# A fused retention and SoLU kernel: the negated row and its maximum taken early for the softmax, squares on ScalarE, new orders

## The chip, the cores and the metric

The kernel runs on one core of a Trainium2 chip. The metric is the device time of one execution in microseconds (us), as the median of repeated runs. The engines are named as in the profile: PE is TensorE's matmul (PEld its weight load), DVE is VectorE, ACT is ScalarE, POOL is GpSimd, and SP is the SyncE queue, which issues nearly all DMAs. SBUF is the working memory on the chip, PSUM the memory into which PE writes.

## The reference

Two layers, one behind the other. The first is a retention layer (8 batches, 8 heads, 576 positions, head size 64), the second a feed-forward layer with a SoLU activation over all 4608 tokens (512 to 1024 to 512):

```
scores = (q @ k.T) / 8                      # per batch and head
ret    = scores * Dmat                      # Dmat[i, j] = gamma_h ** (i - j) for i >= j, else 0
x      = (ret @ v), heads side by side      # 4608 x 512
h      = x @ w_in                           # 4608 x 1024
e      = exp(h - max(h));  sm = e / (sum(e) + 1e-9)
solu   = h * sm
ln     = (solu - mean) / sqrt(var + 1e-6) * g_ln
out    = ln @ w_out                         # 4608 x 512
```

All inputs and outputs are float32.

## The kernel before

**Tiling.** The positions are cut into windows. For each group of four batches there are eight windows of 256 positions (`wi` 0 and 1 of each batch), and one window that holds the last 64 positions of the four batches. That makes 18 windows. Each is worked on twice, for heads 0 to 3 and for heads 4 to 7, which makes 36 *units* (index i). Each window also gives two *token tiles* of 128 tokens, so there are 36 tiles (index t) as well. One unit and one tile make one step of a software pipeline.

**One unit.** SP loads q, k and v as float32 (`ldq`, `ldk`, `ldv`, lines L259 and L266). POOL multiplies q and k by the decay factors and casts them to float16 (`sq`, `sk`, L274) and casts v (`cv`, L282); in the first two units DVE scales q and ACT casts v. PE transposes q and k (`T`, L291), ACT copies them out of PSUM (`qe`, L299). PE forms the scores (`S`, L349), and DVE multiplies them by the causal mask into `ret` (`mask`, L382). The state that goes from chunk to chunk is formed by PE (`K`, L314), two additions on DVE (`sa` and `sd`, L396 to L403), a product and two casts on POOL (`sm` L407, `sc` L416). PE adds the part of earlier chunks (`I`) and of the own chunk (`V`, both L314) in the PSUM tile `xy`, and ACT copies it out as `xT` (`xe`, L422).

**One tile.** PE multiplies xT by w_in into `h_ps`, two banks of PSUM with one buffer (`M1`, L434). ACT takes the exponential and its row sum straight from `h_ps` (`ex`, L447); no maximum is subtracted. DVE multiplies `h_ps` by `e_sb` into `solu` in float16 (`so`, L454), which releases `h_ps`. The softmax's divisor is not divided out: as the layer norm divides by the standard deviation, it only appears in the epsilon. DVE forms mean and variance of `solu` (`bn`, L460 and L464) and, once a window, var + 1e-6 * sum² (L468 and L471, named `w`); POOL raises it to the power -1/2 (`rs`, L477). PE transposes `solu` (`L`, L483), ACT copies it out (`le`, L491), and PE multiplies it by w_out (`M2`, L507). ACT scales the result by `rs` (`oe`, L523) and SP stores it (`out`, L535 and L542).

**The mean.** There are two ways of taking out the mean. Tiles below `NE` (14) use `w2g16`, g times w_out, and DVE corrects the result: `od` (L515) adds the mean times the negative column sums of the weights, `nws`. From tile 14 on, the weights themselves are centred: `w2c16`, made by ACT (`wf`, L657) and POOL (`wp`, L578) in eight pieces, and `od` is left out. The column sums come from a matmul with a matrix of -1 (`WM`, L574), copied out twice by ACT (`nw0`, `nw1`, L665).

**Order.** Each engine works through its queue in order. The order of each queue is written out by hand in `FIRST` for the first part; after that operations come by a due time of period 5.36. `order_ops` merges the five lists into one order of emission, with planned durations from `DUR` and with the number of buffers from `CAP`. Where the plan sees PE idle early on, the kernel emits matmuls on zeros (`wm`, L687 and L694) that keep PE busy.

Of the kernel before, what the change touches and what calls it, by code (L numbers as in the profile page):

```python
# [9 lines left out]
FP = mybir.dt.float32  # L10
F16 = mybir.dt.float16
P = 128
# [4 lines left out]
    qe=0.6, xe=0.59, ex=1.22, le=0.6, oe=0.69, wi=0.6, wg=0.66, cva=0.6,  # L17
    mask=1.22, st_a=0.29, so=1.22, bn=1.68, od=0.7, wib=0.55, wgd=0.5, WM=1.73, nw=0.62, wf=0.66, wp=1.04, sqd=0.7, gc=0.2,
    sq=1.03, sk=1.03, st_b=0.4, cast=0.84, rs=0.6, cv=0.61,
# [6 lines left out]
NE = 14  # L26

FIRST = dict(
    ACT=(
        "cv0 qe0 cv1 qe1 xe0 wi1a wi2a wi0a xe1 wi3a ex0 qe2 wg0 le0 wg2 qe3 wg4 wg6 ex1 xe2 "  # L30
        "nw1 nw0 xe3 qe4 wf1 ex2 qe5 wf3 le1 xe4 qe6 wf2 ex3 le2 xe5 oe0 qe7 wf0 ex4 le3 xe6 "
        "qe8 ex5 le4 xe7 qe9 oe1 ex6 le5 oe2 qe10 xe8 ex7 le6 xe9 qe11 oe3 ex8 le7 oe4 wf6 "
        "qe12 xe10 wf4 ex9 le8 xe11 oe5 wf7 qe13 ex10 le9 xe12 wf5 qe14 oe6 ex11 le10 xe13 "
        "oe7 qe15 oe8 ex12 le11 xe14 qe16 oe9 ex13 le12 xe15 qe17 oe10 ex14 le13"
    ),
    DVE=(
        "gc sq0 sa0 sd0 sq1 mask0 wi1b sa1 sd1 mask1 wi2b wi0b wi3b sa2 sd2 so0 mask2 wg1 sa3 "
        "sd3 wg3 wg5 wg7 mask3 so1 bn0 sa4 sd4 bn1 mask4 so2 od0 sa5 sd5 mask5 bn2 sa6 sd6 "
        "so3 mask6 od1 bn3 sa7 sd7 so4 mask7 od2 bn4 sa8 sd8 so5 mask8 bn5 sa9 sd9 so6 od3 "
        "mask9 bn6 so7 od4 sa10 sd10 mask10 bn7 so8 od5 sa11 sd11 mask11 bn8 sa12 so9 sd12 "  # L40
        "od6 mask12 bn9 sa13 sd13 so10 od7 mask13 bn10 so11 sa14 sd14 od8 bn11 mask14 so12 "
        "sa15 sd15 od9 mask15 bn12 so13 od10 mask16 bn13 so14"
    ),
    PE=(
        "G K0 T0 S0 T1 I0 V0 K1 S1 I1 V1 M1_0 T2 K2 S2 L0 I2 V2 K3 T3 M1_1 S3 WM I3 V3 K4 T4 "
        "M1_2 S4 T5 M2_0 L1 I4 V4 K5 S5 T6 M1_3 I5 V5 K6 S6 L2 M2_1 T7 M1_4 I6 V6 K7 S7 L3 "
        "M2_2 T8 M1_5 I7 V7 K8 S8 L4 M2_3 T9 M1_6 I8 V8 K9 L5 S9 T10 M1_7 L6 I9 M2_4 V9 K10 "
        "S10 T11 M1_8 L7 I10 M2_5 V10 K11 S11 T12 M1_9 L8 I11 V11 K12 S12 M2_6 T13 M1_10 I12 "
        "V12 K13 S13 L9 M2_7 T14 M1_11 I13 L10 M2_8 V13 K14 S14 T15 M1_12 L11 M2_9 I14 V14 "
        "K15 S15 T16 M1_13 L12 I15 S16 V15 M2_10 T17 M1_14 L13 I16 S17 V16 M2_11"  # L50
    ),
    POOL=(
        "sk0 sk1 sm0 sc0 sm1 sc1 sq2 sk2 cv2 sk3 sm2 sc2 cv3 sq3 sm3 sc3 sk4 sq4 cv4 sq5 sk5 "
        "sm4 sc4 sq6 rs0 cv5 sk6 sq7 sm5 sc5 cv6 cv7 sk7 sm6 sk9 sc6 sk8 sq8 wp0 rs1 sm7 sc7 "
        "cv8 sq9 cv10 cv9 wp3 sm8 sk10 sc8 cv12 wp2 sq10 sq11 sq12 sm9 sc9 sk11 cv11 sk12 wp1 "
        "sm10 sc10 sk13 rs2 sq13 sq14 cv14 sm11 sc11 sk14 rs3 wp6 sm12 sc12 cv13 sq16 cv15 "
        "cv16 sm13 sc13 wp4 sk15 sq15 sk16 wp5 rs4 sm14 sc14 sq17 wp7 sk17 rs5 cv17 sm15 sc15 "
        "sq18 sk18 cv18 sq19 sk19 cv19"
    ),
    SP=(  # L60
        "ldk0 ldv0 ldq0 ldk1 ldq1 lm ldv1 lwi1 lwi2 lwi0 lwi3 ldq2 ldk2 ldv2 ldk3 lwo0 ldv3 "
        "ldq3 lwo2 lwo4 lwo6 ldk4 ldq4 ldv4 ldq5 ldk5 ldq6 ldv5 ldk6 ldv7 ldq7 ldq9 ldk7 ldk8 "
        "ldv6 ldq10 ldv8 ldk9 ldq11 ldq8 ldv10 ldk10 ldv11 ldq14 ldk11 ldk14 ldv9 ldv12 ldq12 "
        "ldk12 ldk13 ldq16 out0 out1 ldk17 ldv16 ldq15 ldq13 ldv13 out2 ldv14 ldq17 ldk16 "
        "out4 ldv15 ldk15 out3 out5 out7 out6 ldv17 ldv18 ldq19 ldk18 ldv19 ldq18 ldk19 ldq20 "
        "out8 ldk20 ldv20 out9 ldq21 ldk21 ldv21"
# [107 lines left out]
def kernel(  # L174
# [21 lines left out]
               xT=5, h=1, e=2, oc=2, solu=3, sml=8, lnT=4, o=1, osb=3)  # L196
# [28 lines left out]
    nws = const.tile([P, 2, DM], FP)  # L225
# [213 lines left out]

    def exp_(t):  # L440
        d = tk[t]
        w, c = divmod(t, 2)
        d["e"] = pools["e"].tile([P, DFF], FP, tag="e", name="e_sb")
        if c == 0:
            ws[w]["se"] = pools["sml"].tile([P, 2], FP, tag="se", name="se")
            ws[w]["mv"] = pools["sml"].tile([P, 2, 2], FP, tag="mv", name="mv")
        nc.scalar.activation(  # L447
            out=d["e"], in_=d["h"], func=ACT.Exp, accum_out=ws[w]["se"][:, c : c + 1]
        )

    def solu(t):
        d = tk[t]
        d["solu"] = pools["solu"].tile([P, DFF], F16, tag="solu", name="solu")
        nc.vector.tensor_tensor(out=d["solu"], in0=d["h"], in1=d["e"], op=ALU.mult)  # L454

    def stats(t):
        w, c = divmod(t, 2)
        bs = pools["sml"].tile([P, 2, 6], FP, tag="bs", name="bs")
        for half in range(2):
            nc.vector.bn_stats(  # L460
                out=bs[:, half], in_=tk[t]["solu"][:, half * 512 : half * 512 + 512]
            )
        d = ws[w]
        nc.vector.bn_aggr(out=d["mv"][:, c], in_=bs)  # L464
        if c:
            x = pools["sml"].tile([P, 2], FP, tag="w", name="w")
            d["x2"] = pools["sml"].tile([P, 2], FP, tag="w2", name="w2")
            nc.vector.scalar_tensor_tensor(  # L468
                out=x, in0=d["se"], scalar=1e-6, in1=d["se"], op0=ALU.mult, op1=ALU.mult
            )  # L470
            nc.vector.tensor_tensor(out=d["x2"], in0=x, in1=d["mv"][:, :, 1], op=ALU.add)  # L471
# [39 lines left out]
    def o_mean(t):  # L511

        d = tk[t]
        d["oc"] = pools["oc"].tile([P, DM], FP, tag="oc", name="oc")
        nc.vector.scalar_tensor_tensor(  # L515
            out=d["oc"], in0=nws[:, 0], scalar=ws[t // 2]["mv"][:, t % 2, 0:1], in1=d["o"],
            op0=ALU.mult, op1=ALU.add,
        )
# [58 lines left out]
    def w2_center(x):  # L577
        nc.gpsimd.tensor_tensor(out=w2c16[:, x], in0=w2_f[:, x], in1=nws[:, 1], op=ALU.add)  # L578
# [46 lines left out]
    for t in range(NT):  # L625
        w, c = divmod(t, 2)
        m = t + 2
        op(f"M1_{t}", "PE", "M1", [f"xe{2 * w}", f"xe{2 * w + 1}"] + [f"wi{x}{y}" for x in range(4) for y in "ab"],
           (m, 3.18), lambda t=t: mm1(t), [("h", [f"so{t}"])])
        op(f"ex{t}", "ACT", "ex", [f"M1_{t}"], (m, 5.1), lambda t=t: exp_(t), [("e", [f"so{t}"])])  # L630
        op(f"so{t}", "DVE", "so", [f"ex{t}"], (m + 1, 1.03), lambda t=t: solu(t), [("solu", [f"L{t}", f"bn{t}"])])
        op(f"bn{t}", "DVE", "bn", [f"so{t}", f"bn{t - 1}" if c else ""], (m + 1, 4.5), lambda t=t: stats(t))
        if c:
            op(f"rs{w}", "POOL", "rs", [f"bn{t - 1}", f"bn{t}"], (m + 2, 0.77), lambda w=w: rstd(w), [("sml", [f"oe{t}"])])
        op(f"L{t}", "PE", "L", [f"so{t}"], (m + 1, 4.9), lambda t=t: ln_tp(t), [("tp", [f"le{t}"])])
        op(f"le{t}", "ACT", "le", [f"L{t}"], (m + 2, 0.97), lambda t=t: ln_ev(t), [("lnT", [f"M2_{t}"])])
        o_end = f"od{t}" if t < NE else f"oe{t}"
        op(f"M2_{t}", "PE", "M2", [f"le{t}"] + [f"{'wg' if t < NE else 'wp'}{x}" for x in range(8)], (m + 4, 1.0),
           lambda t=t: mm2(t), [("s" if late(t) else "o", [o_end])])
        if t < NE:  # L640
            op(o_end, "DVE", "od", [f"M2_{t}", "nw0"], (m + 4, 2.9), lambda t=t: o_mean(t), [("oc", [f"oe{t}"])])
        op(f"oe{t}", "ACT", "oe", [o_end if t < NE else f"M2_{t}", f"rs{w}"], (m + 4, 3.6 if t < NE else 2.9),
           lambda t=t: o_ev(t), [("osb", [f"out{t}"])])
        op(f"out{t}", "SP", "out", [f"oe{t}"], (m + 4, 4.4 if t < NE else 3.6), lambda t=t: store(t))
# [8 lines left out]
    op("gc", "DVE", "gc", ["G"], (0, 1.0), lambda: nc.vector.tensor_copy(out=gln, in_=cur["g_ps"][:, 0:8]))  # L653
    for c in range(0, 8, 2):
        op(f"lwo{c}", "SP", "ldw", [], (-2 + c / 8, 0.6), lambda c=c: nc.sync.dma_start(out=w2_f[:, c : c + 2], in_=w2_v[:, c : c + 2]))
        for x in (c, c + 1):
            op(f"wf{x}", "ACT", "wf", ["gc", "nw1"], (8 + x * 0.75, 1.9), lambda x=x: nc.scalar.activation(  # L657
                out=w2_f[:, x], in_=w2_f[:, x], func=ACT.Copy, scale=gln[:, x : x + 1]))
            op(f"wp{x}", "POOL", "wp", [f"wf{x}"], (9 + x * 0.75, 1.9), lambda x=x: w2_center(x))
# [3 lines left out]
    op("WM", "PE", "WM", [f"wg{x}" for x in range(8)], (5, 1.0), w2_sum, [("tp", ["nw0", "nw1"])])  # L663
    for x in range(2):
        op(f"nw{x}", "ACT", "nw", ["WM"], (5, 1.1), lambda x=x: nc.scalar.activation(  # L665
            out=nws[:, x], in_=cur["w_sum"], func=ACT.Copy, scale=1.0 if x == 0 else 1.0 / DFF))
# [7 lines left out]
    with tc.manual_schedule():  # L674
# [4 lines left out]
        nc.vector.memset(minus1, -1.0)  # L679
# [3 lines left out]
        nc.vector.memset(warm, 0.0)  # L683
# [43 lines left out]
```

## Time and profile before

| | us |
|---|---|
| median of 3 runs | 226.4 |
| the runs | 227.62, 225.35, 226.40 |
| span of the profiled execution, first to last instruction | 225.6 |
| PE busy | 208.6 |
| DVE busy | 180.0 |
| POOL busy | 151.6 |
| ACT busy | 133.2 |

The profile gives the span of the one execution that was profiled and no other time of it; the median of the runs lies 0.8 us above that span. Busy times are shares of one engine's own time, overlaps counted once. The mean duration of one instruction can be a little longer than the distance from its start to the next one's: neighbours overlap by some hundredths of a microsecond.

### The profile page before, as it was taken

How to read it: one execution, taken by the hardware profiler on the slowest of the kernel's cores; microseconds unless marked ns; L12 is line 12 of the kernel's file. 1: busy time of each engine (PE TensorE's matmuls, PEld its weight loads, DVE VectorE, ACT ScalarE, POOL GpSimd, SP SyncE). 2: the span in 40 equal slices, each digit the busy share in tenths (PEclk: the TensorE clock that was granted, in tenths of full speed). 3: DMA queues.
4: the chain of work that ended last, by engine and by line, in shares of the span. 5: the costliest groups of instructions: out<-in, count | busy, mean ns of one | idle time of the engine just before them, and what ended most of it. 6: DMA issues, size and time to landing. Idle time of an engine off the chain costs nothing.

```text
span 225.6 us, 7375 instructions
## 1 busy us (share of the span) xinstructions
PE 208.6 (92%) x2983; PEld 122.0 (54%) x2983; DVE 180.0 (80%) x320; ACT 133.2 (59%) x238; POOL 151.6 (67%) x231
## 2 busy tenths in 40 slices
PE   7876989999699999699999999999999999999991
PEld 2423555656355655465665666666566666555440
DVE  6655798999969898999999877778888888876540
ACT  2454776656457876466666566666665556655641
POOL 3439599999959989929669869695968777311010
PEclk9999999999799999999999999999999999999998
DMA  6999999995594600799987777777764552222334
GB/s 178 351 346 346 326 289 289 293 293 135 132 264 109 191 11 3 179 300 310 294 225 202 236 195 205 202 193 193 209 190 107 145 141 53 49 47 60 84 71 117
DMA packets 65635, 42.64 MB, mean 189 GB/s; under 512 B 4024, under 2 KB 59456, under 8 KB 65600
## 3 DMA queue, kind: packets, MB, share of 16 engines
q1 hardware_dynamic: 65200, 41.96, 67.7%
q8 instruction: 23, 0.38, 0.8%
q10 hardware_dynamic: 400, 0.21, 0.6%
q14 instruction: 12, 0.10, 0.2%
HBM read 32.71 MB, written 9.44 MB: 187 GB/s over the span
## 4 chain that ended last, share of the span: by engine, by line
PE 65%; DVE 17%; DMA 5%; POOL 4%; SPq 4%; issue 2%; ACT 1%; DVEq 0%; POOLq 0%; ACTq 0%
PE h_ps L434 22%; PE o_ps L507 21%; PE xy L314 7%; PE tln L483 5%; PE tqk L291 5%; DVE solu L454 4%; PE s_ps L349 4%; DVE bs L460 3%; DVE ret L382 3%; DMA vr<-in_v_dram 3%; SPq L259 3%; DMA masks<-masks 2%; DVE w L471 2%; DVE oc L515 2%; DVE w L468 1%
## 5 line engine op out<-in xcount | busy, mean ns | idle before, releaser
L434 PE MATMUL h_ps<-w_in,xT 128*128 128x512 f16 x288 | 69.7, 386 | 2.0 <-DVE solu L454 1.9
L454 DVE TENSOR_TENSOR solu<-h_ps,e_sb 128x1024 f16<-128x1024 f32 x36 | 43.9, 1219 | 19.2 <-ACT e_sb L447 19.0
L447 ACT ACTIVATE e_sb<-h_ps 128x1024 f32<-128x1024 f32 x36 | 36.8, 1022 | 31.6 <-PE h_ps L434 31.5
L460 DVE BATCH_NORM_STATS2 bs<-solu 128x6 f32<-128x512 f16 x72 | 46.0, 680 | 0.1
L382 DVE TENSOR_TENSOR ret<-s_ps,masks 128x1024 f16<-128x1024 f32 x36 | 43.8, 1215 | 0.2 <-issue 0.2
L434 PEld LDWEIGHTS <-xT 128*128 128x128 f16 x288 | 27.3, 99 | 30.0 <-issue 4.4
L274 POOL TENSOR_TENSOR k<-kr,small 128x512 f16<-128x512 f32 x36 | 37.5, 1041 | 6.9 <-DMA kr<-in_k_dram 5.1
L507 PEld LDWEIGHTS <-lnT 128*128 128x128 f16 x288 | 25.9, 98 | 27.2
L274 POOL TENSOR_TENSOR q<-qr,small 128x512 f16<-128x512 f32 x34 | 35.2, 1039 | 7.0 <-DMA qr<-in_q_dram 6.9
L507 PE MATMUL o_ps<-w2c,lnT 128*128 128x512 f16 x160 | 38.0, 380 | 0.0
L477 POOL TENSOR_TENSOR rs<-w,small 128x2 f32<-128x2 f32 x18 | 12.4, 691 | 30.0 <-DVE w L471 29.9
L299 ACT COPY qkT<-tqk 128x512 f32<-128x512 f32 x36 | 20.9, 580 | 12.6 <-PE tqk L291 12.6
L416 POOL CAST sbd<-g 64x256 f16<-64x256 f32 x64 | 25.6, 400 | 3.3
L507 PE MATMUL o_ps<-w2g,lnT 128*128 128x512 f16 x112 | 26.5, 379 | 0.0
L422 ACT CAST xT<-xy 128x512 f16<-128x512 f32 x36 | 21.4, 593 | 8.1 <-PE xy L314 6.8
L523 ACT ACTIVATE o_sb<-o_ps,rs 128x512 f32<-128x512 f32 x20 | 13.7, 687 | 20.8 <-PE o_ps L507 12.4
L407 POOL TENSOR_TENSOR g<-tt,small 128x128 f32<-128x128 f32 x32 | 13.4, 418 | 16.4 <-DVE tt L403 16.4
L483 PEld LDWEIGHTS <-solu 128*128 128x128 f16 x288 | 18.6, 98 | 9.3 <-DVE solu L454 2.0
L483 PE MATMUL tln<-ident,solu 128*128 128x128 f16 x288 | 22.1, 220 | 1.0 <-DVE solu L454 1.0
L491 ACT COPY lnT<-tln 128x512 f32<-128x512 f32 x36 | 20.8, 579 | 3.5 <-PE tln L483 3.5
L282 POOL CAST v<-vr 128x512 f16<-128x512 f32 x34 | 20.5, 608 | 1.7 <-DMA vr<-in_v_dram 0.3
L314 PE MATMUL xy<-ret,v 64*64 64x128 f16 x576 | 14.6, 219 | 2.0 <-DVE ret L382 2.0
(51 smaller groups left out, 241.7 us busy)
## 6 DMA issues: line engine op xcount, KB each, us to landing
kr<-in_k_dram SPq DMA_DIRECT2D x32, 256.0 KB, 4.9
vr<-in_v_dram SPq DMA_DIRECT2D x32, 256.0 KB, 5.0
qr<-in_q_dram SPq DMA_DIRECT2D x32, 256.0 KB, 4.8
out_dram<-o_sb SPq DMA_DIRECT2D x64, 128.0 KB, 2.4
w_in_f<-in_moe_w_in_dram SPq DMA_DIRECT2D x4, 512.0 KB, 6.8
w_f<-in_moe_w_out_dram SPq DMA_DIRECT2D x4, 512.0 KB, 7.6
qr<-in_q_dram SPq DMA_DIRECT2D x16, 64.0 KB, 2.2
kr<-in_k_dram SPq DMA_DIRECT2D x16, 64.0 KB, 2.7
```

Source lines behind the costliest of these rows:

```text
L274: eng.tensor_tensor(out=t.rearrange("p j h d -> p h j d"), in0=st[i][nm + "r"], in1=g_of(i, base), op=ALU.mult,)
L299: nc.scalar.copy(out=d["qkT"].rearrange("p n h j q -> p (n h j q)").bitcast(FP), in_=d["tp"].rearrange("p n h j q -> p (n h j q)").bitcast ...
L314: nc.tensor.matmul(start=(c, e) not in begun, stop=False, skip_group_check=True, **kw)
L382: nc.vector.tensor_tensor(out=d["ret"].rearrange("p e h j q -> p (e h) (j q)"), in0=d["s"].rearrange("p e h j q -> p (e h) (j q)"), in1=ma ...
L416: nc.gpsimd.tensor_copy(out=s16[ee[e], :, :, ee[e]], in_=st[i]["g"][ee[e]])
L422: nc.scalar.copy(out=d["xT"].rearrange("p c h q -> p c (h q)"), in_=d["av"][:, :, 0:256])
L434: nc.tensor.matmul(out=h_ps[:, hh], lhsT=st[2 * w + dc // 2]["xT"][:, c, dc % 2], rhs=w_in16[:, dc, hh], start=(dc == 0), stop=(dc == 3),)
L447: nc.scalar.activation(out=d["e"], in_=d["h"], func=ACT.Exp, accum_out=ws[w]["se"][:, c : c + 1])
L454: nc.vector.tensor_tensor(out=d["solu"], in0=d["h"], in1=d["e"], op=ALU.mult)
L460: nc.vector.bn_stats(out=bs[:, half], in_=tk[t]["solu"][:, half * 512 : half * 512 + 512])
L483: nc.tensor.transpose(out=tp[:, c], in_=d["solu"][:, c * P : (c + 1) * P], identity=ident)
L507: nc.tensor.matmul(out=d["o"], lhsT=d["lnT"][:, c], rhs=(w2g16 if t < NE else w2c16)[:, c], start=(c == 0), stop=(c == 7))
```

## The change

- `neg_max` (`em`, DVE) is new: it reads `h_ps`, writes -h to `hn` in SBUF (float32, three buffers) and gives the row's minimum of -h as `nm`. It is the last reader of `h_ps`.
- `exp_` reads `hn` with scale -1 and bias `nm`, so that the row's maximum is subtracted.
- `solu` multiplies `hn` by `e_sb` and gives the row sum `su`. Its sign is negative, and so `gln` is negated too.
- `stats` is split: ACT forms the sum of squares about the mean (`squares`, `va`) into `sv`; DVE puts sums together once a window (`x`).
- `NE` goes from 14 to 10, and one copy `nws` serves both uses.
- All five orders in `FIRST` are new and cover the whole run.

```diff
-NE = 14
+NE = 10
+WPOOL = tuple(range(8))
...
-               xT=5, h=1, e=2, oc=2, solu=3, sml=8, lnT=4, o=1, osb=3)
+               xT=5, h=1, hn=3, e=2, oc=2, solu=3, sq=2, sml=8, lnT=4, o=1, osb=3)
...
+    def neg_max(t):
+
+        d = tk[t]
+        d["hn"] = pools["hn"].tile([P, DFF], FP, tag="hn", name="hn")
+        d["nm"] = pools["sml"].tile([P, 1], FP, tag="nm", name="nm")
+        nc.vector.tensor_scalar(
+            out=d["hn"], in0=d["h"], scalar1=-1.0, scalar2=None, op0=ALU.mult, op1=ALU.min,
+            accum_out=d["nm"],
+        )
+
...
         nc.scalar.activation(
-            out=d["e"], in_=d["h"], func=ACT.Exp, accum_out=ws[w]["se"][:, c : c + 1]
+            out=d["e"], in_=d["hn"], func=ACT.Exp, scale=-1.0, bias=d["nm"],
+            accum_out=ws[w]["se"][:, c : c + 1],
         )
...
-        nc.vector.tensor_tensor(out=d["solu"], in0=d["h"], in1=d["e"], op=ALU.mult)
-
-    def stats(t):
...
-            nc.vector.bn_stats(
-                out=bs[:, half], in_=tk[t]["solu"][:, half * 512 : half * 512 + 512]
-            )
...
+        nc.vector.scalar_tensor_tensor(
+            out=d["solu"], in0=d["hn"], scalar=1.0, in1=d["e"], op0=ALU.mult, op1=ALU.mult,
+            accum_out=ws[w]["su"][:, c : c + 1],
+        )
+
+    def squares(t):
+
         w, c = divmod(t, 2)
+        x = pools["sq"].tile([P, DFF], FP, tag="sq", name="sq")
+        nc.scalar.activation(
+            out=x, in_=tk[t]["solu"], func=ACT.Square, scale=-float(DFF),
+            bias=ws[w]["su"][:, c : c + 1], accum_out=ws[w]["sv"][:, c : c + 1],
+        )
...
-           (m, 3.18), lambda t=t: mm1(t), [("h", [f"so{t}"])])
-        op(f"ex{t}", "ACT", "ex", [f"M1_{t}"], (m, 5.1), lambda t=t: exp_(t), [("e", [f"so{t}"])])
...
+           (m, 3.18), lambda t=t: mm1(t), [("h", [f"em{t}"])])
+        op(f"em{t}", "DVE", "em", [f"M1_{t}"], (m, 5.1), lambda t=t: neg_max(t), [("hn", [f"so{t}"])])
+        op(f"ex{t}", "ACT", "ex", [f"em{t}"], (m + 1, 1.1), lambda t=t: exp_(t), [("e", [f"so{t}"])])
```

The end of the new PE order, and of the new order of SP:

```
... I35 V35 S34 L31 M1_33 I34 V34 M2_30 M1_35 M2_31 L33 M1_34 L32 M2_33 L35 M2_32 L34 M2_35 M2_34
... out28 out30 out29 out31 out33 out32 out35 out34
```

## The prediction

> **What bounds the kernel now.** I read the page first, then the busy time by window, the list of waits, the rows of single lines, and the timeline around the odd ones.
>
> ```profile
> span 225.6 us, 7375 instructions
> PE 208.6 (92%) x2983; PEld 122.0 (54%) x2983; DVE 180.0 (80%) x320; ACT 133.2 (59%) x238; POOL 151.6 (67%) x231
> ```
>
> The windows show that the kernel has two phases with different limits (busy us in each, PE first):
>
> ```profile
> 20.00:100.00 80.00, 73.74 (x1134) 43.39 (x1124) 72.57 (x120) 51.75 (x91) 68.49 (x101) 0.98 0.76 204
> 110.00:190.00 80.00, 80.00 (x1247) 49.40 (x1246) 66.94 (x124) 49.04 (x92) 60.45 (x97) 1.00 0.69 187
> ```
>
> From 110 to 190 PE never pauses: one tile each 5.26 us, and DVE (66.9 of 80) and POOL (60.5 of 80) have room. Between 20 and 100 PE loses 6 us, while DVE (72.6) and POOL (68.5) are nearly full. M1_1 starts at 23.9 and M1_14 at 100.9: 5.93 us per tile. All that a change can win lies there, about 0.67 us for each of 13 tiles, and in the tail.
>
> ```profile
> PE h_ps L434 <- DVE solu L454: 1.9, 4, 1.1
> POOL rs L477 <- DVE w L471: 29.9, 11, 8.4
> ```
>
> The wait that an early release of h removes, PE's matmuls into h_ps held by the product at L454, is 1.9 us in all. So the gain has to come from DVE's load, not from h.
>
> The rows that decide my forecast are small ones:
>
> ```profile
> L468 DVE SCALAR_TENSOR_TENSOR w<-se x18: 105/107/1093, 33.0 to 216.4; 128x2 f32<-128x2 f32 x18
> L471 DVE TENSOR_TENSOR w<-w,mv x18: 160/161/1194, 33.1 to 216.6; 128x2 f32<-128x2 f32 x18
> L407 POOL TENSOR_TENSOR g<-tt,small x32: 393/399/848, 8.4 to 191.7; 128x128 f32<-128x128 f32 x32
> ```
>
> Two elements take 107 ns at best and 1093 ns at worst. The timeline shows why:
>
> ```profile
> 55.62 1.27 POOL L578 TENSOR_TENSOR w2c<-w_f,nws 128x512 f16<-128x512 f32 x1
> 55.81 1.09 DVE L468 SCALAR_TENSOR_TENSOR w<-se 128x2 f32<-128x2 f32 x1
> 56.85 3.04 POOL L274 TENSOR_TENSOR q<-qr,small 128x512 f16<-128x512 f32 x3
> 56.94 0.97 DVE L471 TENSOR_TENSOR w<-w,mv 128x2 f32<-128x2 f32 x1
> ```
>
> Each tiny DVE operation ends when the POOL instruction that was running ends. Both of its tensors lie in SBUF. The other way round, at the start:
>
> ```profile
> 7.42 1.04 POOL L274 TENSOR_TENSOR k<-kr,small 128x512 f16<-128x512 f32 x1 [2.00 <-DMA kr<-in_k_dram]
> 8.25 0.76 DVE L274 TENSOR_TENSOR q<-qr,small 128x512 f16<-128x512 f32 x1 [0.48 <-DMA qr<-in_q_dram]
> 8.42 0.85 POOL L407 TENSOR_TENSOR g<-tt,small 128x128 f32<-128x128 f32 x1
> ```
>
> A DVE product of two SBUF tensors runs from 8.25 to 9.01, and the POOL product behind it takes 0.85 instead of 0.40. So on this chip a DVE operation with two SBUF tensors and a POOL operation exclude each other. The big DVE operations of the kernel before (mask L382, solu L454, o_mean L515) each read one tensor from PSUM, and POOL's rows beside them stay at 1.04 (1033 to 1045 over 70 instructions): no exclusion there.
>
> **The change part by part.**
>
> *neg_max (em), 36 new on DVE.* The nearest row is the mask, 128x1024 from PSUM, 1215 ns (started 1.13 apart when back to back). Reading out the accumulator is bounded below by 0 and above by ScalarE's 194 ns read. Below 1.2 it could only go at the rate of the weight casts (430 ns for 512, so 0.86). I take 1.3.
>
> *solu (so).* Before: 1219 ns with h in PSUM. Now h comes negated from hn, so both tensors are in SBUF. Without a collision 1.22 (the clean two-SBUF row is 693 ns for 512 elements), plus the sum's readout, 1.3. With a collision it waits for POOL's running instruction: at least 0, at most 1.27 (w2c). The mean of L468 and L471 above their medians, 0.14 and 0.23, was taken at a POOL load of two thirds; I take 0.35.
>
> [...]
>
> *bn_stats, bn_aggr and two tiny operations go* (2 x 680 + 209 a tile, 249 + 393 a window); two tiny operations a window (x) stay, with the same exposure. DVE per tile without o_mean, in start-to-start times: mask 1.13, em 1.23, so 1.14 + 0.35, state 0.5, x 0.3 = 4.7; the same sum before is 1.13 + 1.14 + 1.3 + 0.13 + 0.5 + 0.3 = 4.5. So DVE gains nothing by the swap. With NE at 10 instead of 14, four o_mean (738 ns) go.
>
> *squares (va), 36 new on ScalarE.* Nearest row: Exp 1022 + 194 readout, starting 1.02 apart when followed at once; a pointer operand costs o_sb (687) against lnT (579) 0.1. Take 1.1, bounds 1.0 to 1.4. ScalarE is 49.0 busy of 80 in the steady window; 15.2 tiles x 1.1 make it 65.7. Hidden by its idle 31 us; at 1.4 it is 70, still hidden. The trace has one table load (1.28 us), and the changed program holds one too, so Square brings none. rs now waits for so, va and x in turn; behind rs on POOL stand scalings and state casts of later units, but POOL reaches rs late when it is the busy one.
>
> *Two nws copies become one, the eight w2 products stay on POOL* (1.27 each). Nothing to gain.
>
> *Start.* The order now puts 21 fill matmuls ahead of T0 (before, four stood ahead of it). The twelve first ones run 0.43 apart until 5.0, later ones 0.215: 33 matmuls end near 10.0, where T0 started at 7.3. By the chain K, state, cast, I, V, xT the first M1 moves from 15.3 to about 18. POOL's sq2 had to wait for its load until 16.6 anyway, and the loads before it are the same 3.9 MB, so POOL loses nothing. If that cover is gone it costs 2.7.
>
> *End.* The last tile stored is now 34, with four DMA issues on SP (six took 2.95, 0.49 each), where the last tile before had two on each of two queues: +1.0.
>
> **The sum.** POOL from sq2 to the state cast of unit 15, which gates M1_14, holds 31 scalings (1.04), 14 casts of v (0.605), 14 state products (0.40), 14 double state casts (0.80), 8 w2 products (1.27), 5 rs (0.69): 71.1 us (before, 71.9 busy in the same stretch). In DVE's order 12 products so stand before that point. What one takes from POOL: the 0.45 lost at 8.42 for 512 elements, doubled, 0.9, up to its whole 1.22; I take 1.0. So 16.6 + 71.1 + 12 = 99.7, and about 2.3 for I15, V15, xT: M1_14 at 102 with no pause of POOL at all. Before, POOL paused for 12.4 us in that stretch (84.3 less 71.9): DMA, sd, rs. POOL is now the one waited for, so I keep half: 6.2. M1_14 at 108.2, against 100.9.
>
> From there the kernel before needed 124.7 us to its end at PE's pace; PE's order after M1_14 is the same but for one more L (0.45), and the tail adds 1.0: 126.1. POOL with the products then fills 60.5 + 15.2 x 1.0 = 75.7 of 80, so it just keeps up. 108.2 + 126.1 = 234.3 against the span of 225.6. The three runs have their median 0.8 above that span, so the forecast is **235 us**.
>
> **The rivals.**
>
> *Convoy, slower still.* Each so waits a whole POOL operation (1.04) and mask and em queue behind it: DVE per tile 1.13 + 1.23 + 2.18 + 0.5 + 0.3 = 5.3, plus 0.67 with o_mean. 20 + 10 x 6.0 + 26 x 5.3 + 2.8 (weight casts) + 10 (tail) = 231 without a pause; with the 6.2 twice over and the late start added, 246. For it: the 1093 and 1194 in the rows. Against: their means.
>
> *Faster.* The exclusion costs little, because POOL idles for 35 us between 16.6 and 195 and the products fall into these pauses. Then PE bounds all tiles: M1 at 18.2, and up to M1_14 its order has 14 M1 and 10 M2 and WM at 1.73, one M2 more, 12 L and 16 T at 0.45, 14 to 15 of I, V, S, K at 1.08: 73, and 4 us of early pauses: 95.2; 95.2 + 126.1 = 221.3, so 222 us. It decides if the products meet POOL so rarely that less than 3 us of the 12 are lost. Against: POOL is 68.5 busy of 80 just there.
>
> *The release of h pays nothing and the costs cancel.* Half of the 12 and of the pauses: 226 to 228, no change.
>
> **How the numbers follow.** POOL and product in turns (229 to 241): 0.50. Convoy (241 to 265, the long end for a slow product): 0.22. Faster (218 to 224): 0.17. Cancelled: 0.11. About 1% can be told from no change here. Slower by over 1%: 0.75; within 1%: 0.08; faster: 0.17. 221 to 250 leaves out some 0.06 below and 0.12 above; the forecast's own range is 229 to 241.
>
> **What would show it.** Right: so above 1.4 us on average, with a wide spread; POOL's scalings no longer all at 1.04; POOL busy near 185, since a blocked row is drawn out as at 8.42; PE idle for over 20 us; M1_14 after 104. Wrong: so near 1.25 with no spread, POOL's rows unchanged, M1_14 at 95 to 98. If so is over 2 us even beside an idle POOL, the product itself is slow and not the exclusion. If ScalarE sits before PE in the chain, squares were not hidden.

## The result, and the profile after

The changed kernel takes 244.7 us (median of 4 runs, 244.07 to 246.13) against 226.8 us, the median of four runs of the kernel before: ratio 1.082, 95% interval 1.075 to 1.088. The forecast was 235 us, with a range of its own of 229 to 241 and of 221 to 250 with its rivals. The direction and the exclusion came as written; the loss is 8.2% where 3.8% was forecast, and most of the difference comes from the second half of the run.

The head of the page and the same two windows as before (per window: length, then busy us of PE, PEld, DVE, ACT and POOL):

```profile
span 242.0 us, 7430 instructions
PE 212.7 (88%) x2999; PEld 122.5 (51%) x2999; DVE 177.0 (73%) x316; ACT 176.6 (73%) x309; POOL 178.2 (74%) x231
...
20.00:100.00 80.00, 68.79 (x1047) 40.42 (x1045) 67.14 (x110) 61.46 (x107) 73.09 (x91) 1.00 0.78 217
110.00:190.00 80.00, 74.06 (x1142) 44.42 (x1140) 61.47 (x110) 63.08 (x112) 67.19 (x86) 1.00 0.64 177
```

POOL has the same 231 instructions and is busy 26.6 us longer. PE, which never paused between 110 and 190, now loses 6 of 80 us there. DVE is no fuller than before in either window, so it is not DVE's load that costs.

The rows of single lines (count, then shortest, median and longest in ns): the product, its readout, and POOL's products and casts.

```profile
L500 DVE SCALAR_TENSOR_TENSOR solu<-hn,e_sb x36: 1207/1316/2297, 23.9 to 231.6; 128x1024 f16<-128x1024 f32 x36
L500 DVE DVE_READ_ACCUMULATOR solu<-hn,e_sb x36: 75/77/83, 25.2 to 232.8; 128x1 f32 x36
...
L307 POOL TENSOR_TENSOR k<-kr,small x36: 1036/1042/2017, 6.5 to 204.7; 128x512 f16<-128x512 f32 x36
L307 POOL TENSOR_TENSOR q<-qr,small x34: 1034/1042/2019, 16.5 to 203.1; 128x512 f16<-128x512 f32 x34
...
L449 POOL CAST sbd<-g x64: 389/398/1395, 12.2 to 213.3; 64x256 f16<-64x256 f32 x64
```

POOL's scalings, which all lay between 1033 and 1045 ns before, now reach 2019. The timeline shows one exchange in full (start, duration, engine and line; only POOL's instructions and DVE's two products are shown):

```profile
117.68 1.04 POOL L307 TENSOR_TENSOR q<-qr,small 128x512 f16<-128x512 f32 x1
118.00 1.80 DVE L500 SCALAR_TENSOR_TENSOR solu<-hn,e_sb 128x1024 f16<-128x1024 f32 x1
118.66 1.61 POOL L315 CAST v<-vr 128x512 f16<-128x512 f32 x1
119.73 1.62 DVE L500 SCALAR_TENSOR_TENSOR solu<-hn,e_sb 128x1024 f16<-128x1024 f32 x1
120.24 2.02 POOL L307 TENSOR_TENSOR k<-kr,small 128x512 f16<-128x512 f32 x1
```

A first product starts at 118.00 while POOL scales q, and lasts 1.80; POOL's cast of v behind it takes 1.61 instead of its usual 0.61. The second product starts at 119.73, while that cast still runs to 120.27, and ends at about 121.3. POOL's next scaling begins at 120.24, stands still until the product is done, and then takes its usual 1.04: 121.3 + 1.0 = 122.3, the 2.02 shown. In this exchange the two engines work in turns.

The chain of work that ended last, by engine:

```profile
PE 34%; POOL 32%; DVE 13%; ACT 7%; issue 5%; DMA 4%; SPq 2%; POOLq 0%; DVEq 0%; ACTq 0%
```

A third of it is POOL. Where PE waits for POOL is seen in the waits: for the state casts.

```profile
PEld L347 <- POOL sbd L449: 15.4, 15, 2.3
PE xy L347 <- POOL sbd L449: 9.4, 13, 1.6
```

Before, the same two waits were 3.5 and 2.2 us. The weight loads (PEld) wait at the same moments as the matmuls, so the two can't be added: PE itself waits 9.4 us. Most of that lies ahead of M1_14, the first matmul of tile 14. From there to the end these are PE's longest waits:

```profile
PE xy L347 <- POOL k L307: 2.4, 1, 2.4
PE xy L347 <- POOL sbd L449: 2.1, 6, 0.5
PE xy L347 <- POOL v L315: 1.2, 1, 1.2
```

**Where the 16.4 us of span lie.** From the timeline of PE, the start of each tile's first matmul into `h_ps`:

| us | M1_0 | M1_1 | M1_14 | M1_14 to end | M1_1 to end | span |
|---|---|---|---|---|---|---|
| before | 15.3 | 23.9 | 100.9 | 124.7 | 201.7 | 225.6 |
| forecast | 18 | | 108.2 | 126.1 | | 234.3 |
| after | 19.2 | 22.5 | 107.3 | 134.7 | 219.5 | 242.0 |

The first stretch came within 1 us of the forecast. The stretch behind M1_14 took 8.6 us more than forecast. M1_0 is late, but M1_1 is early; from M1_1 on the changed kernel loses 17.8 us. (The 201.7 of before hold some 1.7 us of a lower clock: its granted clock was 0.79 between 56 and 64, and eight matmuls into `h_ps` took 3.56 us there, 1.90 as a rule.) The busy times of the stretch behind M1_14, before and then after:

```profile
100.90:225.60 124.70, 119.08 (x1668) 71.05 (x1665) 95.77 (x171) 72.46 (x132) 73.84 (x114) 0.99 0.60 161
107.30:242.00 134.70, 122.33 (x1675) 70.85 (x1672) 92.28 (x168) 104.16 (x183) 89.22 (x116) 0.99 0.51 138
```

Of its 10.0 extra us, 3.2 are PE shown busy for longer and 6.8 are PE idle (12.4 against 5.6). POOL is 89.2 busy of 134.7: not full, and yet waited for.

### The profile page after: what moved, and what is told of

The parts are those of the page before. It is cut to its first block, busy times and chain, and to the rows that moved or that the text cites. A ratio compares the mean times of both kernels' runs of the same rounds, so it can differ in the third digit from the quotient of the medians.

```text
span 242.0 us, 7430 instructions
## 1 busy us (share of the span) xinstructions
PE 212.7 (88%) x2999; PEld 122.5 (51%) x2999; DVE 177.0 (73%) x316; ACT 176.6 (73%) x309; POOL 178.2 (74%) x231
## 4 chain that ended last, share of the span: by engine, by line
PE 34%; POOL 32%; DVE 13%; ACT 7%; issue 5%; DMA 4%; SPq 2%; POOLq 0%; DVEq 0%; ACTq 0%
PE h_ps L467 10%; POOL q L307 8%; POOL sbd L449 8%; PE o_ps L559 7%; POOL k L307 5%; PE xy L347 4%; POOL g L440 4%; POOL rs L529 3%; PE tln L535 3%; PE tqk L324 3%; DVE solu L500 3%; DVE hn L478 2%; POOL w2c L631 2%; DVE ret L415 2%; DMA out_dram<-o_sb 2%
## 5 line engine op out<-in xcount | busy, mean ns | idle before, releaser
L500 DVE SCALAR_TENSOR_TENSOR solu<-hn,e_sb 128x1024 f16<-128x1024 f32 x36 | 51.1, 1427 | 7.3 <-ACT e_sb L490 7.3
L478 DVE TENSOR_SCALAR_CACHE_REDUCE hn<-h_ps 128x1024 f32<-128x1024 f32 x36 | 43.8, 1218 | 12.7 <-PE h_ps L467 12.4
L307 POOL TENSOR_TENSOR k<-kr,small 128x512 f16<-128x512 f32 x36 | 42.1, 1173 | 10.0 <-DMA kr<-in_k_dram 7.8
L559 PE MATMUL o_ps<-w2c,lnT 128*128 128x512 f16 x192 | 45.4, 379 | 0.0
L509 ACT ACTIVATE sq<-solu,su 128x1024 f32<-128x1024 f16 x36 | 41.4, 1152 | 2.8 <-DVE solu L500 2.6
L490 ACT ACTIVATE e_sb<-hn,nm 128x1024 f32<-128x1024 f32 x36 | 41.4, 1150 | 0.6 <-DVE hn L478 0.5
L467 PEld LDWEIGHTS <-xT 128*128 128x128 f16 x288 | 26.6, 98 | 29.5 <-DVE gln L712 1.8
L307 POOL TENSOR_TENSOR q<-qr,small 128x512 f16<-128x512 f32 x34 | 39.0, 1154 | 2.1 <-DMA qr<-in_q_dram 1.0
L449 POOL CAST sbd<-g 64x256 f16<-64x256 f32 x64 | 32.9, 514 | 3.1
L455 ACT CAST xT<-xy 128x512 f16<-128x512 f32 x36 | 21.0, 584 | 19.0 <-PE xy L347 15.3
L529 POOL TENSOR_TENSOR rs<-w,small 128x2 f32<-128x2 f32 x18 | 17.9, 992 | 21.2 <-DVE w L521 20.9
L347 PE MATMUL xy<-qkT,sbd 128*128 128x128 f16 (+1 forms) x128 | 13.6, 214 | 11.6 <-POOL sbd L449 9.4
L535 PEld LDWEIGHTS <-solu 128*128 128x128 f16 x288 | 17.8, 98 | 8.6 <-issue 2.1
L575 ACT ACTIVATE o_sb<-o_ps,rs 128x512 f32<-128x512 f32 x24 | 16.5, 686 | 7.8 <-POOL rs L529 3.2
```

Source lines behind the costliest of these rows:

```text
L307: eng.tensor_tensor(out=t.rearrange("p j h d -> p h j d"), in0=st[i][nm + "r"], in1=g_of(i, base), op=ALU.mult,)
L449: nc.gpsimd.tensor_copy(out=s16[ee[e], :, :, ee[e]], in_=st[i]["g"][ee[e]])
L467: nc.tensor.matmul(out=h_ps[:, hh], lhsT=st[2 * w + dc // 2]["xT"][:, c, dc % 2], rhs=w_in16[:, dc, hh], start=(dc == 0), stop=(dc == 3),)
L478: nc.vector.tensor_scalar(out=d["hn"], in0=d["h"], scalar1=-1.0, scalar2=None, op0=ALU.mult, op1=ALU.min, accum_out=d["nm"],)
L490: nc.scalar.activation(out=d["e"], in_=d["hn"], func=ACT.Exp, scale=-1.0, bias=d["nm"], accum_out=ws[w]["se"][:, c : c + 1],)
L500: nc.vector.scalar_tensor_tensor(out=d["solu"], in0=d["hn"], scalar=1.0, in1=d["e"], op0=ALU.mult, op1=ALU.mult, accum_out=ws[w]["su"][:, ...
```

## The experiments

My theory: the products and POOL work in turns, and that is the loss. The rivals: ScalarE's squares, DVE's new `neg_max`, the late start, or the new written orders. In the results, "behind M1_14" is the time from M1_14 to the end of the span; ratios are to the kernel before, with 95% intervals. "From M1_1" is the time from the start of tile 1's M1 to the end of the span.

**1. The changed kernel with a product of one source.**

```diff
-        nc.vector.scalar_tensor_tensor(
-            out=d["solu"], in0=d["hn"], scalar=1.0, in1=d["e"], op0=ALU.mult, op1=ALU.mult,
+        nc.vector.tensor_scalar(
+            out=d["solu"], in0=d["e"], scalar1=-1.0, scalar2=None, op0=ALU.mult, op1=ALU.add,
             accum_out=ws[w]["su"][:, c : c + 1],
```

> The changed kernel, with the product's place taken by a DVE operation on e alone (e times -1, with its row sum): same engine, same size, same order, but one tensor in SBUF instead of two. The product with h is left out. Theory (exclusion between DVE's product and POOL): POOL's scalings go back to 1.04 us each, POOL busy from 178 to about 152, M1_14 from 107 to 95 to 100, and from M1_14 to the end 125 to 128 instead of 134.7: 221 to 229 us. Rival 1 (ScalarE's new load is what costs): 241 to 245. Rival 2 (the new orders cost, with their pairs of tiles): POOL's rows are short again, but the time stays at 237 or more.

Ratio 1.041 (1.035 to 1.047); span 233.7, M1_14 at 101.4, 132.3 behind it. POOL is back at its old busy time and the spread is gone from its rows:

```profile
PE 214.7 (92%) x2999; PEld 124.0 (53%) x2999; DVE 170.0 (73%) x316; ACT 176.2 (75%) x309; POOL 151.5 (65%) x231
...
L500 DVE TENSOR_SCALAR_CACHE_REDUCE solu<-e_sb x36: 1204/1212/1222, 26.6 to 223.3; 128x1024 f16<-128x1024 f32 x36
...
L307 POOL TENSOR_TENSOR k<-kr,small x36: 1035/1042/1221, 6.5 to 196.8; 128x512 f16<-128x512 f32 x36
```

An operation with one SBUF source of the same size takes 1212 ns, as the two-source product does when nothing blocks it (1207 at the shortest). So the product itself is not slow.

The span falls by 8.3 of the 16.4 us, but that is too little. This execution is 2.5 us late before the edit can act: its first product starts at 26.6, and M1_1 stands at 25.2, against 22.5 in the changed kernel and 22.7 in run 4, which runs the same instructions up to there. PE was slower at the start (its first twelve fill matmuls took 5.30 us, in run 4 4.34) and in M1_0, where the granted clock stands at 7 tenths in the profile's slice from 17.5 to 23.4. M1_0 and the granted clock over the span in tenths, here and then in run 4:

```profile
20.30 3.43 PE L467 MATMUL h_ps<-w_in,xT 128*128 128x512 f16 x8 [1.33 <-DVE gln L712]
PEclk9997999999999999999999999999999799999998
...
19.34 1.90 PE L467 MATMUL h_ps<-w_in,xT 128*128 128x512 f16 x8 [1.33 <-DVE gln L712]
PEclk9999999999999999999999999999999799999999
```

All four executions here show a mean clock of 0.981 to 0.983, those of run 4 0.990 and 0.992, so the ratio holds it too; without it the ratio would be an estimated 1.03 (236.0 less 2.5, over 227.1). From M1_1 the kernel takes 208.5 us, against 219.5 with the second source and 201.7 before. So the second source costs 11.0 of the 17.8 us. Between M1_1 and M1_14 nothing of the loss is left (84.7 us with it, 76.2 without, 77.1 before). What is left lies behind M1_14 and has another cause.

**2. The kernel before with two SBUF sources.** The counter-test: only the exclusion is added.

```diff
-        nc.vector.tensor_tensor(out=d["solu"], in0=d["h"], in1=d["e"], op=ALU.mult)
+        nc.vector.tensor_tensor(out=d["solu"], in0=d["e"], in1=d["e"], op=ALU.mult)
```

> The kernel before with one edit: its product reads e twice (e times e) in place of h and e, so that both tensors lie in SBUF; the product with h is left out, and h is released by the exponential. Orders, ScalarE's load and DVE's durations stay. Exclusion theory: POOL's rows are stretched by some 0.7 us per product, 25 us in all, the product waits for POOL too, and the time is 232 to 242. Both rivals: 224 to 228, with h released early.

Ratio 1.048 (1.041 to 1.055).

```profile
L454 DVE TENSOR_TENSOR solu<-e_sb x36: 1170/1288/1926, 20.1 to 223.8; 128x1024 f16<-128x1024 f32 x36
...
L274 POOL TENSOR_TENSOR k<-kr,small x36: 1032/1041/2022, 3.9 to 202.1; 128x512 f16<-128x512 f32 x36
...
20.00:100.00 80.00, 70.96 (x1069) 41.51 (x1063) 67.86 (x112) 48.73 (x86) 75.88 (x95) 0.96 0.68 186
110.00:190.00 80.00, 79.31 (x1236) 48.86 (x1233) 70.94 (x122) 48.85 (x90) 67.63 (x90) 1.00 0.71 193
```

The same signature appears, POOL is busy 177.4 in all, and M1_14 moves from 100.9 to 110.2 (from M1_1 to M1_14 it is 84.9 us instead of 77.1). But behind M1_14 the cost is only 0.9 (125.6 against 124.7): PE keeps its pace there, just as the prediction assumed. So the exclusion alone does not break that stretch; the changed kernel has something more.

**3. Squares on 8 of 1024 columns**, in the changed kernel, and **4. both** (this and the product of one source).

```diff
-            out=x, in_=tk[t]["solu"], func=ACT.Square, ...
+            out=x[:, 0:8], in_=tk[t]["solu"][:, 0:8], func=ACT.Square, ...
```

> The changed kernel with the squares cut to 8 of 1024 columns, which takes some 0.95 us of ScalarE from each tile, 34 us in all; the variance is left out with it. Exclusion theory: 240 to 245, as ScalarE is hidden. Rival 1 (ScalarE's load): 226 to 234, with ScalarE's waiters (qkT, xT, lnT) gone from the chain. Rival 2 (orders): 240 to 245.

> Both of these: the operation on e alone, and squares of 8 columns. What is left over the kernel before is due to the orders, the start and neg_max. Exclusion theory: within 2 us of the one-source run, 221 to 228. Rival 1: 222 to 230, and at least 8 below the one-source run. Rival 2: 235 or more.

Squares alone: 1.091 (1.082 to 1.100), no gain. Both: 1.025 (1.017 to 1.034), where the one-source product alone gave 1.041. Of the 3.5 us of span between these two, 2.5 are the late M1_1 of run 1, which lies ahead of its first squares (28.1). From M1_1 it is 207.5 against 208.5. So ScalarE's squares are hidden as long as POOL is waited for, and are worth some 1.0 us when it is not. Behind M1_14 still 131.9.

**5. One source and `neg_max` on 8 columns**, exp reading a tile of weights instead.

```diff
-            out=d["hn"], in0=d["h"], scalar1=-1.0, ...
+            out=d["hn"][:, 0:8], in0=d["h"][:, 0:8], scalar1=-1.0, ...
...
-            out=d["e"], in_=d["hn"], func=ACT.Exp, scale=-1.0, bias=d["nm"],
+            out=d["e"], in_=w_in_f[:, 0], func=ACT.Exp, scale=-1.0, bias=d["nm"],
```

> The one-source run (236 us, 132.3 from M1_14 to the end) with neg_max cut to 8 of 1024 columns; it still releases h. The exponential reads a float32 tile of weights of the same size instead of hn, and the product with h and the full maximum are left out. If neg_max's 1.2 us on DVE is what holds the last two thirds: 125 to 128 from M1_14 to the end, 224 to 230 in all. If the written orders hold them: 130 or more, 232 to 237.

Ratio 1.028 (1.022 to 1.034); from M1_1 207.6, and 131.9 behind M1_14 once more. Its windows:

```profile
20.00:100.00 80.00, 75.81 (x1175) 45.09 (x1173) 55.57 (x123) 65.96 (x117) 70.56 (x103) 1.00 0.83 233
110.00:190.00 80.00, 76.09 (x1156) 45.35 (x1155) 43.45 (x111) 61.69 (x109) 53.60 (x87) 0.98 0.63 172
```

With DVE at 43 of 80 and POOL at 54 of 80, PE still loses 4 us. No engine's load explains that. The longest pause is one of 2.3 us before 177.4, in which PE waits for POOL's scaling of k, and that for its load; the eight matmuls of the next M1 then took 2.94 us instead of 1.90:

```profile
176.26 1.04 POOL L307 TENSOR_TENSOR k<-kr,small 128x512 f16<-128x512 f32 x1 [2.26 <-DMA kr<-in_k_dram]
...
178.06 2.94 PE L467 MATMUL h_ps<-w_in,xT 128*128 128x512 f16 x8
```

Run 1 has the same pause (2.8 us, before 180.5, and then 2.97 for the eight matmuls), and the changed kernel one of 2.4. So the order in which the engines and the loads work is the next suspect.

**6. Orders by due time from M1_14 on**, with the changed dataflow in full, and **7. the same with one source.**

```diff
+CUT = dict(ACT="ex14", DVE="so13", PE="M2_11", POOL="cv17", SP="ldk18")
+FIRST = {e: x[: x.index(f" {CUT[e]} ") + len(CUT[e]) + 1] for e, x in FIRST.items()}
```

> The changed kernel with its written orders cut off near M1_14 (ACT after ex14, DVE after so13, PE after M2_11, POOL after cv17, SP after ldk18); what comes later goes by due time with a period of 5.36, as in the kernel before. Product, squares and exclusion stay. From M1_14 to the end the changed kernel took 134.7 us, the kernel before 124.7, and the kernel before with a product of two SBUF tensors 125.6. Theory A (in this stretch the written order with its paired tiles is what costs, not the exclusion): 125 to 129 here, 233 to 238 in all. Theory B (neg_max lengthens the way from M1 to the product, or squares load ScalarE, whatever the order): 132 or more here, 241 to 247 in all.

> The changed kernel in due-time order from M1_14 on (as in the run of that name, which took 140.0 us from M1_14 to the end) and with the operation on e alone in the product's place; the product with h is left out. If in the due-time order the exclusion alone makes the stretch long: 124 to 127 us from M1_14 to the end, M1_14 near 101, 226 to 231 in all. If neg_max on the way from M1 to the product makes it long: 132 to 138, 235 to 242.

The window of 110 to 190, first with the exclusion, then without:

```profile
110.00:190.00 80.00, 71.45 (x1080) 42.95 (x1079) 60.11 (x105) 63.90 (x112) 59.46 (x82) 1.00 0.62 168
```

```profile
110.00:190.00 80.00, 79.73 (x1230) 48.12 (x1219) 60.09 (x119) 67.76 (x119) 60.09 (x94) 1.00 0.62 167
```

With the exclusion 1.101 (1.097 to 1.105) and 140.0 behind M1_14: worse than the written orders. Without it 1.019 (1.013 to 1.024), 129.9, between what its two theories asked for, and PE works 79.7 of 80 us. Two things follow. The written orders themselves cost time when nothing excludes anything: 2.4 us behind M1_14 (132.3 less 129.9). They don't explain all of it: 129.9 is still 5.2 us more than before, with PE idle 3.0 us longer and busy 2.2 us longer. And in the due-time order the exclusion alone is worth 10.1 us behind M1_14 (140.0 less 129.9), in the written orders 2.4 (134.7 less 132.3, which has the slower matmuls behind its pause in it), in the old dataflow 0.9.

This price does not follow what POOL loses. Behind M1_14 the exclusion adds 9.3 us to POOL's busy time in the due-time order (83.9 against 74.6), 15.1 in the written orders (89.2 against 74.1) and 9.3 in the old dataflow (83.1 against 73.8). What goes with it is how long PE waits there for state casts: 1.0 us in run 2, 2.1 in the changed kernel, none shown in run 7, and 7.8 in run 6:

```profile
PE xy L349 <- POOL sbd L451: 7.8, 12, 0.9
```

**8. SP's order alone by due time** (with one source), **9. SP's and POOL's**, **10. SP's alone in the full change**, and **11. one source, small squares and SP's order together.** The edit is that of 6 with only `SP="ldk18"`, or with `SP` and `POOL`, in `CUT`.

> The changed kernel with solu reading e alone (no exclusion; the product with h is left out), and the order of SP's queue written out only as far as ldk18, by due time from there; the orders of the other four engines stay. With solu reading e alone and all orders as written, M1_14 stood at 101.4 and 132.3 us followed it; with all five orders by due time 129.9 followed it. Theory A, the loads stand in the wrong order on SP, POOL waits for kr and the rest follows: 124 to 129 after M1_14, ratio to the kernel before 1.00 to 1.025. Theory B, POOL's own order (sm before its additions, rs before its sums) holds it: SP's order alone changes less than 1.5, 131 to 134 after M1_14, ratio 1.03 to 1.05. Theory C, the five orders fit each other and any one alone makes it worse: over 134, ratio above 1.05.

> As the last, and POOL's order too is written out only as far as cv17 and goes by due time from there; ScalarE's, DVE's and PE's orders stay as written. Theory A (SP's loads): as with SP alone, within 1.5 of it. Theory B (POOL's own order): 124 to 130 after M1_14, ratio 1.00 to 1.03, and POOL's waits for tt (L436) and for w (L521) fall from 22.6 to under 10 in 108 to 215. Theory C (the orders of PE, DVE and ACT hold it): 131 to 135 after M1_14, the waits of POOL merely move.

> The changed kernel in full, with the order of SP's queue written out only as far as ldk18 and by due time from there; nothing else differs. With solu reading e alone the same cut took 5.4 us off the span (233.7 to 228.3). Theory A, the price of SP's written order is independent of the exclusion: it comes off here too, span 236 to 238, M1_14 near 104.5, ratio to the kernel before 1.05 to 1.065. Theory B, POOL's lost time hides it (POOL is the one waited for, so loads are early enough): span 240 to 243, ratio 1.07 to 1.085. Theory C, the due order collides with the longer POOL rows as the five due orders did: over 244.

> Three parts taken out at once: solu reads e alone, the squares run on 8 of 1024 columns, and SP's order is by due time from ldk18 on; the product with h and the variance are left out. neg_max, exp from hn, the late start and the orders of the other four engines stay. Exclusion, ScalarE and SP's order were worth 8.3, 3.5 and 5.4 us of span one after the other. If the three add up: span 224 to 227, ratio 0.995 to 1.01, and what is left over the kernel before is within about 1 us. If ScalarE and SP's order are the same wait seen twice: span 227.5 to 230, ratio 1.01 to 1.025.

| | M1_1 | M1_14 | behind it | from M1_1 | ratio |
|---|---|---|---|---|---|
| one source (1) | 25.2 | 101.4 | 132.3 | 208.5 | 1.041 (1.035 to 1.047) |
| and SP by due time (8) | 22.8 | 98.6 | 129.7 | 205.6 | 1.025 (1.016 to 1.033) |
| and SP and POOL (9) | 22.9 | 99.0 | 141.9 | 218.0 | 1.073 (1.066 to 1.079) |
| full change, SP by due time (10) | 23.4 | 108.2 | 136.8 | 221.6 | 1.091 (1.085 to 1.097) |
| one source, small squares, SP (11) | 25.7 | 101.0 | 129.4 | 204.8 | 1.018 (1.011 to 1.024) |

Run 11's profiled execution has the same late M1_1 as run 1 (M1_0 took 3.59 us), and it lay 1.9 us above its median; so the times from M1_1 are the ones to compare.

Without the exclusion SP's order is worth 2.9 us from M1_1 (208.5 to 205.6), 2.6 of it behind M1_14. POOL's wait for `kr` after 100, 7.0 us in the one-source kernel, is gone, and so is PE's pause of 2.8 us with the 2.97 us of matmuls behind it. This lies between theories A and B, and is part of what is left, not all of it. POOL's order by due time among written ones makes it much worse, so the orders can't be exchanged one by one at will. In the full change SP's order saves nothing (1.091 against 1.082; the intervals overlap a little).

The three parts do add up, once all are counted from M1_1: the second source 11.0, the squares 1.0 and SP's order 2.9 make 14.9 us, and run 11 lies 14.7 below the changed kernel (204.8 against 219.5). The expectation of 0.995 to 1.01 was missed because its 3.5 and its 5.4 us of span both held the 2.5 us of run 1's late start.

**12. The early start in the full change, and 13. in the kernel of 7.** Three fill matmuls instead of 21 ahead of T0.

```diff
+START_PE = 6.5
...
-    end_pe, fill = 0.0, True
+    end_pe, fill = START_PE, True
```

> The changed kernel with 3 fill matmuls ahead of T0 instead of 21; nothing else differs. If the start is on the path: M1_0 at 16 to 17 instead of 19.2, and 1 to 3 us less in all, 241.5 to 244. If loads and POOL set the first tiles anyway: M1_0 earlier, M1_3 and the time unchanged, 244 to 246. If PE then starts cold: first matmuls twice as long and no gain.

> The changed kernel with solu reading e alone and all five orders by due time from M1_14's neighbourhood on (ratio 1.0187 with M1_0 at 19.1), now with three fill matmuls ahead of T0 instead of 21, so that M1_0 starts near 16. Theory A, the late start is what is left: M1_14 near 96.5, ratio 1.00 to 1.01. Theory B, the start is given back behind it, as it was with the exclusion on: M1_14 98 to 99.5, ratio 1.014 to 1.022, and what is left lies in the order around M1_14 and in the tail.

In the full change M1_0 comes at 15.9 instead of 19.2 and M1_14 at 105.3, but the end does not move: 1.081 (1.076 to 1.086). With one source and due-time orders M1_0 moves from 19.1 to 16.7, M1_14 from 99.2 to 97.0, and the ratio falls from 1.019 to 1.009 (1.006 to 1.012).

This gives a ledger, in which each step holds all earlier ones: full change 1.082; one source 1.041; orders by due time 1.019; early start 1.009. Of the step from 1.041 to 1.019, about half is not the orders but run 1's late M1_1 (2.5 of 5.3 us); from M1_1 the orders are worth 1.9 us (208.5 to 206.6). The remaining 0.9% I didn't take apart. Taken alone in the full change, neither the orders (1.101) nor the start (1.081) gain anything.

**14. The kernel before with the product from PSUM and squares on ScalarE.** The row sum comes out of the product, `bn` goes, `h` stays in PSUM, no maximum; old written orders with `va` put behind `le`.

```diff
-        nc.vector.tensor_tensor(out=d["solu"], in0=d["h"], in1=d["e"], op=ALU.mult)
+        nc.vector.scalar_tensor_tensor(
+            out=d["solu"], in0=d["h"], scalar=1.0, in1=d["e"], op0=ALU.mult, op1=ALU.mult,
+            accum_out=ws[w]["su"][:, c : c + 1],
+        )
```

> The kernel before with one idea of the change and without neg_max: the product reads h from PSUM and e from SBUF and gives its own row sum, the squares go to ScalarE, bn_stats and bn_aggr are gone; the old orders with the squares put in behind lnT's copies. No maximum is subtracted, as before. Exclusion theory: the product stays at 1.2 to 1.3 us and POOL's rows at 1.04; DVE loses 1.4 us per tile, so the first phase goes from 5.93 us per tile towards 5.3: M1_14 at 92 to 97 and 217 to 223 us. If ScalarE's load is the trouble: M1_14 at 100 or later and 226 to 232.

**15. The same with the written orders cut near M1_3.**

```diff
+CUT = dict(ACT="ex2", DVE="mask4", PE="L1", POOL="cv4", SP="ldk6")
+FIRST = {e: x[: x.index(f" {CUT[e]} ") + len(CUT[e]) + 1] for e, x in FIRST.items()}
```

> The run with the product from PSUM and the squares on ScalarE (230.6 us; M1_14 at 105.9, then 125.0) with the written orders cut off already near M1_3 (ACT after ex2, DVE after mask4, PE after L1, POOL after cv4, SP after ldk6), so that the due-time order, which kept PE full from M1_14 on there, also serves the tiles before. If the written order, made for another load, was what held the first stretch: M1_14 at 93 to 100, 219 to 226 in all. If loads or POOL hold it: M1_14 at 104 or later, 230 or more.

With the old written order 1.016 (1.011 to 1.021), where 217 to 223 us had been expected and 230.6 came: M1_14 at 105.9 (in an execution 2.1 us above its median), but 125.0 behind it. With that order cut, 224.1 us, ratio 0.991 (0.988 to 0.995), M1_14 at 98.4 and 124.0 behind it: 0.9% less than the kernel before. The kernel before was not run with its own orders cut there, so how much of this is the squares and how much the order is open.

```profile
PE 206.3 (93%) x2983; PEld 121.6 (55%) x2983; DVE 132.1 (59%) x248; ACT 172.1 (77%) x310; POOL 152.2 (68%) x231
...
110.00:190.00 80.00, 80.00 (x1247) 49.23 (x1246) 50.29 (x93) 65.94 (x121) 62.83 (x100) 1.00 0.64 172
```

Squares on ScalarE and a row sum out of the product take 48 us off DVE (180.0 to 132.1) and cost no pace of PE. So what made the change slow is not this part of it by itself.

## Why the prediction was right or wrong

**DVE, `neg_max` at 1.3:** right (1218 ns and a readout of 82). **The product at 1.3 and a wait of 0.35:** a little high; 1427 mean and a readout of 77, so 1.50. DVE gained nothing, as forecast, and had room all the same.

**The product isn't slow by itself:** right: 1207 ns at best for 1024 float32 elements with a row sum, and 1214 where POOL ran nothing beside it (at 209.2), against 1212 for one source (run 1).

**POOL loses 1.0 for each product:** the mechanism is shown by runs 1 and 2 in both directions, and the size was right where the forecast used it. From sq2 to the state cast of unit 15 POOL is busy 80.6 us in the changed kernel and 69.1 without the exclusion (run 4): 11.5 for 12 products, 0.96 each. Behind M1_14 24 products take 15.1, 0.63 each; over all 36 it is 0.74.

**M1_14 at 108.2:** measured 107.3, and right term by term: sq2 at 16.5 (forecast 16.6), POOL's work without the products 69.1 (71.1), the products 11.5 (12), pauses 7.1 (6.2), from the cast to M1_14 3.1 (2.3). The pauses came out partly by luck. The 12.4 us that were halved run from 16.6 up to M1_14 itself; up to the state cast at 97.3, which is the stretch of the sum, the kernel before paused for 9.2, and half of that is 4.6.

**Squares hidden by ScalarE's idle time:** right in the changed kernel (run 3); where POOL is no longer in the way they cost some 1.0 us (run 4). The forecast took 1.1 for one; it is 1152 ns. It also left exp at 1022, though its input moved from PSUM to SBUF and it got a pointer for a bias: 1150 ns, 4.6 us more of ScalarE over 36 tiles.

**Start +3 and no loss for POOL:** M1_0 at 19.2 instead of 18, with 1.3 us in which PE waited for DVE's `gln` (L712), which no term held. M1_1 was 1.4 us earlier than before, and run 12 shows that the delay costs nothing in the changed kernel. Its cover is POOL; without it the start is worth 1% (run 13).

**Tail +1.0:** 0.8 (15.7 from the last tile's M1, 14.9 before).

**"From there the kernel before needed 124.7 us … POOL just keeps up":** this is the step that failed, 134.7 instead of 126.1. It put two costs behind M1_14 at nothing. The first is the exclusion: POOL at 75.7 of 80 us was to suffice. POOL was in fact only 67.2 busy, and PE waited for it still, because a load below 80 doesn't say when an instruction ends: from M1_14 on PE waits 2.4 us for one scaling of k, 2.1 for state casts and 1.2 for a cast of v. Without the exclusion the stretch is 2.4 us shorter (run 1).

The second and larger cost is everything else that is new there. I compared PE's queue alone, but ScalarE's, DVE's, POOL's and SP's were new too, and PE's pace is what all five give together. With neither exclusion nor squares, or nearly without `neg_max`, the stretch still takes 131.9 (runs 4 and 5), 5.8 more than the forecast had with the exclusion. Of the 8.6 us, 2.4 are the second source (run 1), 2.9 the squares and SP's written order together (run 11, 129.4, with the second source out), and for the other 3.3 the cause stays open.

The rest of the miss is a conversion. I added 0.8 from span to time, the distance between the median of three runs and the span of one of them. In every execution on record the time is 1.7 to 2.1 us above its own span, and the median here is 2.7 above the profiled span: 1.9 of the 9.7 us between 235 and 244.7.

**The rivals.** The convoy asked for 2.18 per product on DVE; it was 1.50, so the time between my forecast and the convoy's 246 did not come from there. No run shows the slow product that its range up to 265 stood for; the product's shortest here is 1207 ns, and the slowest kernel on record took 249.3 us (run 6). The faster case needed under 3 us of loss ahead of M1_14; run 1 shows 8.5 between M1_1 and M1_14 (84.7 to 76.2).

**What stays open.** Why the exclusion costs 0.9 behind M1_14 in the old dataflow and 10.1 in the new one with due-time orders, though POOL loses 9.3 us to it in both. The new path from M1 to `solu` has one more station (`em`), which could leave less slack; no run isolates that. Open too are the 3.3 us behind M1_14 that no run accounts for, and why PE's clock is low at the start in some executions and not in others.

## What to carry to other kernels

Before an operand is moved from PSUM to SBUF to free a bank early, look at who shares the time with its reader: here a second SBUF source on DVE took 0.74 us per product from a GpSimd that PE waited for, while the bank had been worth 1.9 us in all. The price of a wait that is hidden is not zero but conditional: squares, late start and load order each saved nothing beside POOL's loss, and once it was gone 1.0, 2.2 and 2.9 us. Count such prices from the point where an edit first acts: over the whole span, a slow start of 2.5 us in run 1 passed for the gain of two later edits. When a change moves work between engines, compare all queues, and try the plain periodic order beside the written one (1.016 against 0.991 in the last two runs).

## What the runs showed of the hardware

- A float32 product of two SBUF tensors with a row sum, 128x1024, took 1214 ns where POOL ran nothing beside it (at 209.2) and 1207 at its shortest, an operation with one SBUF source 1212 as a median (run 1).
- DVE's readout of an accumulator took 77 (`solu`) and 82 ns (`hn`) as medians, ScalarE's 192.
- Exp of 128x1024 from SBUF with a pointer bias took 1150 ns against 1022 from PSUM without. The 128 ns between them hold the move to SBUF and the pointer together; no run here separates the two.
- One product stretched to 2297 ns beside a w2 product of 1272 on POOL (1.09 us above the shortest product), and a cast on POOL of usually 398 ns to 1395 beside a product (1.00 us more).
- With the same instructions up to there, the eight matmuls of M1_0 took 3.43 us in run 1 and 1.90 in run 4, with the granted clock at 7 and at 9 tenths in the profile's slice that holds its start (17.5 to 23.4 and 17.3 to 23.0).
